# Two score levels of a chunked RWKV-6 kernel computed in 32 by 32 and 64 by 64 blocks of the TensorE array

## The chip, the cores and the metric

The kernel runs on one core of a Trainium2 chip. The metric is the device time of one launch in microseconds; lower is better. The kernel before takes 628.2 us (median of three runs, 627.67 to 628.48). Everything is float32.

## What is computed

The reference is an RWKV-6 attention followed by a small feed-forward block:

```python
# r, k, v, w: (4 batches, 8 heads, 768 tokens, 48)
for t in range(S):
    cur   = einsum('bhd,bhe->bhde', u * k[t], v[t])
    y[t]  = einsum('bhd,bhde->bhe', r[t], state + cur)
    state = w[t] * state + einsum('bhd,bhe->bhde', k[t], v[t])
x   = y, heads side by side            # (3072, 384)
h   = x @ w_in                         # (3072, 2048)
out = (h * sigmoid(h)) @ w_out         # (3072, 384)
```

The recurrence is not run token by token. Inside a chunk of 128 tokens the weight of key j for query t is the product of r[t], k[j] and all decays w between them. The kernel builds the 128 x 128 matrix of these scores level by level. At level l the chunk is cut into blocks of c = 2^l tokens. A block of odd number has its queries scored against the keys of the even block just before it, with queries and keys already multiplied by the decays up to the border between the two blocks. Level 0 and the diagonal come by another way; levels 1 to 6 are matrix products on TensorE.

## The kernel before

**Units.** The work is cut into 12 units, each of 128 tokens of two batches (`units`, six chunks times two pairs of batches). The eight heads of a batch are four pairs (`NP = 4`); of a pair, one head's 48 channels lie in partitions 0 to 47 and the other's in partitions 64 to 111 (the loop `for e in range(2)` with `rows = slice(PD * e, PD * e + D)`). The second batch of a unit is kept with its tokens in reverse order in places, so that the keys of both batches that a level needs stand in one set of 128 columns (`X[l % 2] + p`): even blocks from batch 0, odd positions from the reversed batch 1.

**Scores.** `score_products` (L659 to L673, its product at L669) makes one level. For each pair p and each half e it issues one product: the stationary operand is 48 x 128 (all 128 keys), the moving one 48 x 128 (64 queries of each batch, taken with a stride, since only the odd blocks count). That is eight products for a level. The result is 128 keys x 128 columns, of which only the blocks where key and query block belong together are scores; the rest is thrown away. `keep_masked` (L676 to L680) then writes the wanted elements into `score` with one predicated copy of 128 x 512 on VectorE for each half, four for two levels.

**Bursts.** From the third unit on, two neighbouring levels are computed back to back: `prepare` makes a second copy of the queries ahead, and `burst` (L743) issues level l from the older queries and level l+1 from the newer. `burst(i, 3)` makes levels 3 and 4, `burst(i, 5)` makes levels 5 and 6. `keep_level` (L751) follows for each of the two levels, then `go_on`, which grows keys (GpSimd) and queries (VectorE) for the next step. The results stay in two pairs of PSUM buffers (`p_sc` and `p_m`, in the third unit `p_sc` and `p_o`). `scores` (L682 and after) is the form of the first two units, where levels are made one at a time; it also knows a copy of rectangles in place of a masked one, on ScalarE, for the levels listed in `COPIED` (L698).

**The rest of a unit.** `turn_k` (L781) transposes keys, `y_state` (L794), `y` (L807) and `update` (L821) make the outputs and the new state, `up` (L929) and `quarter` (L995) are the feed-forward products of the units before. `y` reads `score` and so waits for the copies of all levels.

**Order.** The order is written out by hand: `mix(i)` gives groups of attention steps of unit i, and the main loop puts a counted number of feed-forward steps (`downs(i-2) + ups(i-1)`) behind each group. Every engine then runs its own instructions in the order of the code. A float32 product appears in the profile as two pairs of a weight load and a matmul, so eight products of a level are 16 records of each kind.

Of the kernel before, what the change touches and what calls it, by code (L numbers as in the profile page):

```python
# [38 lines left out]
def kernel(  # L39
# [11 lines left out]
    nc = tc.nc  # L51

    B, H, S, D = r.shape
    DM, DF = moe_w_in.shape
    L = 128
    NL = 7
    NB = 2
    NP = H // 2
    PD = 64
    Q = NB * NP  # L60
    NX = Q + 2 * NP
    X = 0, NP + Q
# [5 lines left out]
    NTOK = 2  # L68
# [250 lines left out]
    NSC = 1  # L319
    score = const.tile([128, NSC, 2, Q, L], F32, name="score")  # L320

    masks = {}
    first = {}
    for l in range(NL):
        c, ni = 1 << l, L >> (l + 1)
# [18 lines left out]
    tw, tr, tk, diag, kq, xt = {}, {}, {}, {}, {}, {}  # L344
# [311 lines left out]
        start_keys(i, nc.gpsimd, False)  # L656


    COPIED = (0, 5, 0), (0, 6, 0), (1, 6, 0)  # L659

    def score_products(i, l, queries, sc):
        c, ni = 1 << l, L >> (l + 1)

        for p in range(NP):
            for e in range(2):
                rows = slice(PD * e, PD * e + D)

                apart, r_p, s_p = 2 * (NP - p) - 1, queries[rows, p, :], sc[e][:, p, :]
                nc.tensor.matmul(bass.AP(tensor=s_p.tensor, offset=s_p.offset,  # L669
                                         ap=[s_p.ap[0], [apart * L // 2, 2], [1, L // 2]]),  # L670
                                 lhsT=tk[i][rows, X[l % 2] + p, :],
                                 rhs=bass.AP(tensor=r_p.tensor, offset=r_p.offset + c,
                                             ap=[r_p.ap[0], [apart * L, 2], [2 * c, ni], [1, c]]),  # L673
                                 start=True, stop=True)

    def keep_masked(i, l, e, sc):  # L676
        c, ni = 1 << l, L >> (l + 1)
        dst = score[:, i % NSC, e].rearrange("p (b q) (i s c) -> p b q i s c", b=NB, s=2, c=c)[:, :, :, :, 1, :]
        nc.vector.copy_predicated(out=dst, mask=masks[l][:, :, None].to_broadcast([128, NB, NP, ni, c]),  # L679
                                  data=sc[e].rearrange("p (b q) (i c) -> p b q i c", b=NB, c=c))  # L680

    def scores(i, l, *between):  # L682
        c, ni = 1 << l, L >> (l + 1)

        name = "p_h" if i == 0 and l % 2 == 1 else "p_sc"
        sc = [ps.tile([128, Q, L // 2], F32, name=name, bufs=2) for e in range(2)]
        score_products(i, l, tr[i], sc)
        if i < NTOK and l + 2 < NL:
            odd_keys(i, l + 1)

        def keep(e):
            if (i, l, e) in COPIED:

                for b in range(NB):
                    for x in range(ni):
                        first = 2 * x * c if b == 0 else L - (2 * x + 1) * c
                        rows, columns = slice(first, first + c), slice((2 * x + 1) * c, (2 * x + 2) * c)
                        nc.scalar.copy(out=score[rows, i % NSC, e, b * NP:(b + 1) * NP, columns],  # L698
                                       in_=sc[e][rows, b * NP:(b + 1) * NP, x * c:(x + 1) * c])
                return  # L700
            keep_masked(i, l, e, sc)
# [39 lines left out]
    made = {}  # L741

    def burst(i, l):  # L743

        other = (second[0], "p_o") if i == NTOK else (ps, "p_m")
        for x, (pool, name) in enumerate(((ps, "p_sc"), other)):
            made[i, l + x] = [pool.tile([128, Q, L // 2], F32, name=name, bufs=2) for e in range(2)]
        score_products(i, l, before.pop((i, l)), made[i, l])
        score_products(i, l + 1, tr[i], made[i, l + 1])

    def keep_level(i, l):  # L751
        for e in range(2):
            keep_masked(i, l, e, made[i, l])

    def go_on(i, l):

# [110 lines left out]
    def mix(i):  # L867
# [22 lines left out]
        if i < NPAIR:  # L890
            groups = [[*both(turn, i, "w"), (product, i, 0)],
                      [*both(turn, i, "k"), *both(turn, i, "r"), (odd_ones, i)], [(start_levels, i), (prepare_keys, i, 1)],
                      [(prepare, i, 1), *[(product, i, l) for l in range(1, NL)]],
                      [(burst, i, 1), (keep_level, i, 1)],
                      [(keep_level, i, 2), (go_on, i, 2)],
                      [(prepare, i, 3), (reverse_v, i), (bonus, i, 0)],
                      [(burst, i, 3), (keep_level, i, 3), (bonus_sum, i, 0), (bonus, i, 1), (bonus, i, 2)],
                      [(keep_level, i, 4), (go_on, i, 4), (bonus_sum, i, 1), (load_rk, i + 1), (load_u,)],
                      [(prepare, i, 5), (make_block_mask,), (bonus_spread, i), (bonus_write, i)],
                      [(burst, i, 5), (keep_level, i, 5), (keep_level, i, 6), (go_on, i, 6)], *end]  # L900
        else:
            groups = [[], [(odd_keys, i, 2), (grow_keys, i, 2, False), (grow_queries, i, 2), *sum_steps(i, 2)],
                      [(prepare, i, 3), *bonus_steps(i, 6, 7)],
                      [(burst, i, 3), (keep_level, i, 3), *sum_steps(i, 3, 4), (block_move, i), *at(ahead, (load_rk, i + 1))],
                      [(keep_level, i, 4), (go_on, i, 4)],
                      [(prepare, i, 5), (reverse_v, i)],
                      [(block_spread, i), (block_write, i)],
                      [(burst, i, 5), (keep_level, i, 5), (keep_level, i, 6), (go_on, i, 6)], *end]
# [231 lines left out]
```

## Time and profile before

| | |
|---|---|
| median of the runs | 628.2 us (627.67 to 628.48) |
| the profiled execution | 628.39 us |
| its span | 626.6 us |
| around the span | 1.8 us (628.39 - 626.6) |
| TensorE busy in the span | 620.3 us, 99% |
| VectorE busy | 438.6 us, 70% |
| GpSimd busy | 363.7 us, 58% |
| ScalarE busy | 187.4 us, 30% |
| granted TensorE clock | full, in every slice |

The span is the time from the first to the last instruction that the profiler saw; the launch adds 1.8 us to it. In lists of groups a line holds the source line, the engine, the operation, the tiles written and read, the shape, the number of instructions, their busy time and the mean of one, and the idle time of the engine ahead of them. Matmul records overlap, so the mean duration of one matmul is its latency; its price in a stream is the time of a stretch divided by the number of its matmuls, which the chain of waits gives.

### The profile page before, as it was taken

Reading aid. Unit: us, or ns where it says so; the run is one execution under the profiler, and the core shown is the slowest. Engines: PE = TensorE matmul, PEld = TensorE weight load, DVE = VectorE, ACT = ScalarE, POOL = GpSimd, SP = SyncE. Lnnn points to the kernel's source line nnn. Section 1 sums busy time; section 2 is a strip of 40 time slices with the busy share of each in tenths; the row PEclk is TensorE's granted clock in tenths of the full one; section 3 lists DMA queues with packets and bytes.
Section 4 is the critical chain, followed back from the end, with each engine's and each line's share of the span. In section 5 each row is a group of like instructions: output and inputs, shape, how many; then the busy total and the mean of one; then the engine's idle time right before and its main releaser. Section 6 shows DMA issues by size and latency. Waiting matters only on the chain.

```text
span 626.6 us, 12324 instructions
## 1 busy us (share of the span) xinstructions
PE 620.3 (99%) x4606; PEld 562.8 (90%) x4606; DVE 438.6 (70%) x749; ACT 187.4 (30%) x380; POOL 363.7 (58%) x414
## 2 busy tenths in 40 slices
PE   8999999999999999999999999999999999999997
PEld 8888876799899899899899899889889989989997
DVE  6879779898995694794794595686596596571041
ACT  6798882221321320320320321221221221220110
POOL 6998388566676567567577378378378458400000
PEclk9999999999999999999999999999999999999999
DMA  9966874443543643543543543542542312100000
GB/s 227 291 154 163 164 203 49 88 79 66 101 68 50 133 66 68 106 69 63 105 67 54 110 65 52 115 64 51 115 70 50 77 33 51 35 1 27 25 1 25
DMA packets 203067, 53.25 MB, mean 85 GB/s; under 512 B 186752, under 2 KB 194816, under 8 KB 203008
## 3 DMA queue, kind: packets, MB, share of 16 engines
q1 hardware_dynamic: 201424, 51.88, 41.1%
q10 hardware_dynamic: 1584, 0.59, 0.4%
q8 instruction: 36, 0.59, 0.4%
q14 instruction: 23, 0.19, 0.1%
HBM read 43.21 MB, written 5.24 MB: 77 GB/s over the span
## 4 chain that ended last, share of the span: by engine, by line
PE 94%; POOL 1%; DVE 1%; ACT 1%; DMA 1%; issue 1%; POOLq 0%; ACTq 0%
PE p_h L929 41%; PE p_o L995 32%; PE p_sc L669 5%; PE p_m L951 3%; PE p_m L807 3%; PE p_m L794 3%; PE p_m L669 3%; PE p_m L781 1%; PE p_sc L821 1%; DMA raw<-in_k_dram 1%; PE p_m L372 1%; POOL tk L625 1%; PE p_m L845 0%; DVE score L584 0%; POOL w_in_sb L241 0%
## 5 line engine op out<-in xcount | busy, mean ns | idle before, releaser
L929 PE MATMUL p_h<-xt,w_in_sb 128*128 128x256 f32 x1152 | 258.1, 382 | 0.7 <-POOL tk L649 0.7
L929 PEld LDWEIGHTS p_h<-xt,w_in_sb 128*128 128x128 f32 x1152 | 215.9, 190 | 32.6 <-POOL tk L649 0.9
L938 ACT ACTIVATE gt<-p_h 128x512 f32<-128x512 f32 x90 | 53.7, 597 | 256.1 <-PE p_h L929 255.9
L625 POOL TENSOR_TENSOR tk<-tk,tw 128x256 f32<-128x256 f32 x128 | 88.7, 714 | 62.4 <-ACT tk L595 34.7
L995 PE MATMUL p_o<-own,temps 128*128 128x192 f32 x528 | 87.9, 326 | 0.0
L995 PE MATMUL p_o<-w_out_sb,gt 128*128 128x192 f32 x508 | 87.3, 328 | 0.0
L995 PEld LDWEIGHTS p_o<-own,temps 128*128 128x128 f32 x528 | 86.0, 190 | 0.2
L995 PEld LDWEIGHTS p_o<-w_out_sb,gt 128*128 128x128 f32 x508 | 82.7, 190 | 0.9 <-issue 0.4
L487 POOL TENSOR_TENSOR ruk<-tokens_rk 128x768 f32<-128x768 f32 (+1 forms) x32 | 48.5, 1527 | 46.3 <-DMA tokens_rk<-in_k_dram 33.7
L977 DVE TENSOR_TENSOR temps<-gt 128x256 f32<-128x256 f32 x84 | 55.4, 660 | 18.3 <-ACT gt L938 18.3
L408 POOL TENSOR_TENSOR tw<-tw 128x256 f32<-128x256 f32 (+6 forms) x83 | 43.8, 528 | 40.2 <-DVE tw L360 36.3
L679 DVE COPY_PREDICATED score<-mask,p_sc 128x512 f32<-128x512 int8 x62 | 44.5, 772 | 13.4 <-PE p_sc L669 12.7
L607 DVE TENSOR_TENSOR tr<-tr,tw 128x512 f32<-128x512 f32 x61 | 49.6, 813 | 3.7 <-POOL tk L625 1.1
L595 ACT COPY tk<-tk 128x256 f32<-128x256 f32 x52 | 20.9, 403 | 85.4 <-POOL tk L625 67.1
L1004 DVE TENSOR_TENSOR partial<-p_o,partial 128x192 f32<-128x192 f32 x33 | 11.8, 358 | 47.2 <-PE p_o L995 47.1
L669 PEld LDWEIGHTS p_sc<-tr,tk 48*128 48x128 f32 x512 | 31.4, 187 | 10.3 <-issue 7.3
L669 PE MATMUL p_sc<-tr,tk 48*128 48x128 f32 x512 | 37.7, 285 | 0.7 <-POOL tk L625 0.6
L1004 DVE TENSOR_TENSOR temps<-p_o,partial 128x192 f32<-128x192 f32 x22 | 7.9, 358 | 33.3 <-PE p_o L995 23.1
L995 PE MATMUL p_o<-w_out_sb,temps 128*128 128x192 f32 x176 | 30.4, 326 | 0.0
L995 PEld LDWEIGHTS p_o<-w_out_sb,temps 128*128 128x128 f32 x176 | 28.9, 190 | 0.0
L487 POOL TENSOR_TENSOR tokens_rk<-tokens_rk,tokens_w 128x192 f32<-128x192 f32 (+1 forms) x32 | 26.8, 857 | 1.3
L977 DVE TENSOR_TENSOR temps<-temps,gt 128x256 f32<-128x256 f32 x43 | 25.7, 598 | 1.5
(170 smaller groups left out, 828.0 us busy)
## 6 DMA issues: line engine op xcount, KB each, us to landing
w_out_sb<-in_moe_w_in_dram SPq DMA_DIRECT2D x6, 768.0 KB, 7.0
w_out_sb<-in_moe_w_out_dram SPq DMA_DIRECT2D x4, 768.0 KB, 5.1
own<-in_moe_w_out_dram SPq DMA_DIRECT2D x4, 768.0 KB, 5.1
tokens_rk<-in_r_dram SPq DMA_DIRECT2D x8, 384.0 KB, 4.5
tokens_rk<-in_k_dram SPq DMA_DIRECT2D x8, 384.0 KB, 5.3
tokens_w<-in_w_dram SPq DMA_DIRECT2D x8, 384.0 KB, 6.6
xt<-yt SPq DMA_DIRECT2D x60, 48.0 KB, 2.0
raw<-in_w_dram SPq DMA_DIRECT2D x80, 32.0 KB, 2.3
```

The source lines that it names most:

```text
L408: engine.tensor_tensor(out=up, in0=t[:, :, 0::2], in1=t[:, :, 1::2], op=ALU.mult)
L487: mul = lambda out, one, two: nc.gpsimd.tensor_tensor(out=out, in0=one, in1=two, op=ALU.mult)
L595: nc.scalar.copy(out=keys(i, X[(l + 1) % 2] * L + c, [4 * c, blocks], [c, 2], [1, c]), in_=keys(i, NP * L + c, [4 * c, blocks], [NP * L + ...
L607: nc.vector.tensor_tensor(out=odd, in0=odd, in1=tw[i][l][:, :, 0::2][:, :, :, None].to_broadcast([128, Q, L >> (l + 1), c]), op=ALU.mult)
L625: nc.gpsimd.tensor_tensor(out=out, in0=have, in1=odd_products(i, l, b, *blocks), op=ALU.mult)
L669: nc.tensor.matmul(bass.AP(tensor=s_p.tensor, offset=s_p.offset, ap=[s_p.ap[0], [apart * L // 2, 2], [1, L // 2]]), lhsT=tk[i][rows, X[l % ...
L679: nc.vector.copy_predicated(out=dst, mask=masks[l][:, :, None].to_broadcast([128, NB, NP, ni, c]), data=sc[e].rearrange("p (b q) (i c) -> ...
L929: nc.tensor.matmul(p_h[:, a, :], lhsT=w_in_sb[:, c, f * 128:(f + 1) * 128], rhs=xt[i][:, c, :], start=(c == 0), stop=(c == KC - 1))
L938: nc.scalar.activation(out=gt[i, m], in_=p_h, func=AF.Silu)
L977: nc.vector.tensor_tensor(out=out, in0=one, in1=two, op=op)
L995: nc.tensor.matmul(p, lhsT=left(f), rhs=right[:, f, :], start=(f == 0), stop=(f == FH - 1))
L1004: nc.vector.tensor_tensor(out=to, in0=p, in1=known, op=ALU.add)
```

## The change

For units from the third on and levels from 5 on, `score_products` no longer multiplies all 128 keys with all queries and masks the result. It walks over the blocks of keys (four of 32 at level 5, two of 64 at level 6) and multiplies each with the one block of queries that belongs to it: a stationary operand of 48 x 32 (48 x 64) and a moving one of the same size, written to the 32 (64) partitions of PSUM that belong to these keys. `corner` tells for block x which batch it belongs to and where its tokens begin. The products of level 5 become 32 in place of 8, those of level 6 become 16 in place of 8. `keep_level` no longer calls the masked copy for these levels; since the wanted elements now are rectangles, it copies each rectangle for all four pairs at once: half e = 0 on VectorE, half e = 1 on ScalarE, four copies of 32 x 128 for level 5 and two of 64 x 256 for level 6 on each of the two engines. The first two units and levels 1 to 4 are as they were.

```diff
+    APART = 5
+
+    def corner(l, x):
+
+        return x % 2, x if x % 2 == 0 else (L >> l) - 1 - x
+
     COPIED = (0, 5, 0), (0, 6, 0), (1, 6, 0)
 
     def score_products(i, l, queries, sc):
         c, ni = 1 << l, L >> (l + 1)
+        if i >= NTOK and l >= APART:
+            for p in range(NP):
+                for x in range(L // c):
+                    b, first = corner(l, x)
+                    q = (p, 2 * NP - 1 - p)[b]
+                    for e in range(2):
+                        rows = slice(PD * e, PD * e + D)
+                        nc.tensor.matmul(sc[e][x * c:(x + 1) * c, q, first // 2 * c:(first // 2 + 1) * c],
+                                         lhsT=tk[i][rows, X[l % 2] + p, x * c:(x + 1) * c],
+                                         rhs=queries[rows, q, (first + 1) * c:(first + 2) * c], start=True, stop=True)
+            return
 
         for p in range(NP):
...
     def keep_level(i, l):
+        c = 1 << l
         for e in range(2):
-            keep_masked(i, l, e, made[i, l])
+            if l < APART:
+                keep_masked(i, l, e, made[i, l])
+                continue
+            for x in range(L // c):
+                b, first = corner(l, x)
+                (nc.vector.tensor_copy if e == 0 else nc.scalar.copy)(
+                    out=score[x * c:(x + 1) * c, i % NSC, e, b * NP:(b + 1) * NP, (first + 1) * c:(first + 2) * c],
+                    in_=made[i, l][e][x * c:(x + 1) * c, b * NP:(b + 1) * NP, first // 2 * c:(first // 2 + 1) * c])
```

## The prediction

> **What bounds the kernel now.** I read the page first (busy shares, clock, the chain by engine), then the list of waits of TensorE, then the chain in order of time around the units.
>
> ```profile
> PE 620.3 (99%) x4606; PEld 562.8 (90%) x4606; DVE 438.6 (70%) x749; ACT 187.4 (30%) x380; POOL 363.7 (58%) x414
> PEclk9999999999999999999999999999999999999999
> PE 94%; POOL 1%; DVE 1%; ACT 1%; DMA 1%; issue 1%; POOLq 0%; ACTq 0%
> ```
>
> TensorE (PE) carries 94% of the chain, at full clock. The list of its waits says whether it ever stands still for another engine:
>
> ```profile
> PE p_m L1030 <- POOL ident masks.py:199: 1.4, 1, 1.4
> PE p_h L929 <- POOL tk L649: 0.7, 1, 0.7
> PE p_sc L669 <- POOL tk L625: 0.6, 1, 0.6
> PE p_m L372 <- ACT tr L384: 0.2, 1, 0.2
> PE p_m L372 <- DMA raw<-in_k_dram: 0.2, 1, 0.2
> ```
>
> Five waits, each once, 3.1 us in all, and all in the first two units. From the third unit on, where the change acts, TensorE never waits for data. So the kernel is worth what TensorE's own instructions cost, and time that the change takes out of them leaves the end of the kernel. Their prices come from the chain (start, duration, work; x counts records, two for a product):
>
> ```profile
> 50.36 1.09 PE p_sc L669 x16
> 51.45 2.79 PE p_h L929 x12
> ...
> 456.55 1.09 PE p_sc L669 x16
> 457.64 0.89 PE p_m L669 x16
> 458.54 5.38 PE p_h L929 x24
> 463.91 0.87 PE p_m L781 x8
> 464.79 2.59 PE p_h L929 x12
> 467.38 1.78 PE p_m L794 x16
> 469.16 1.89 PE p_m L807 x32
> 471.05 0.72 PE p_sc L821 x32
> ```
>
> The two L669 lines at 456.55 are the levels 5 and 6 of one unit: 1.09 + 0.89 = 1.98 us. The same pair stands in the chain once for each of the 10 units from the third on. Four readings follow.
> - A record of 256 columns costs 2.59 / 12 = 216 ns, one of 128 (L794) 111 ns: about 0.83 ns a column and 5 ns.
> - Two blocks of the array work side by side. L669 uses the upper and the lower rows in turn: 0.89 / 16 = 56 ns a record, half of 111. L807 and L821 use two groups of output columns in turn: 59 ns for 128 columns, and 0.72 / 32 = 22.5 ns for 48 columns, where one block alone would need 45.
> - A change between shapes of the array costs 0.2 us each way: the first level of a burst takes 1.09 and the second 0.89; twelve L929 records take 2.79 after scores and 2.59 after transposes. In the timeline the next weight load starts about 0.09 us after the last stream before it would have ended, and the first matmul waits about 0.11 us for its 128 columns of weights.
> - Issue. By narrowing the timeline's window, the two records of a pair of blocks start 6 to 7 ns apart (441.348 and 441.355). The sequencer is quicker than any stream here: two of its own waits, both behind an emptied queue, stand at 46.34 and 46.51, with 14 records (28 instructions) between them.
>
> ```profile
> L669 PEldq EVENT_SEMAPHORE  x1: 51/51/51, 46.3 to 46.3; - x1
> L929 PEldq EVENT_SEMAPHORE  x1: 51/51/51, 46.5 to 46.5; - x1
> ```
>
> That is 165 - 51 = 114 ns for 28 instructions, 4 ns each, 8 ns for a weight load and its matmul.
>
> [...]
>
> **The change part by part.** All of it for one unit, times 10.
>
> *Removed on TensorE:* 32 records of L669, 1.98 us.
>
> *Level 5 added:* 32 products, 64 records, 48 x 32 with 32 columns, over 8 blocks (two row groups, four column groups). By the array each block has 8 records of 0.83 x 32 + 5 = 32 ns: 0.26 us. By issue 64 records: at 6.5 ns 0.42 us, at the sequencer's 8 ns 0.51 us, at L821's 22.5 ns 1.44 us. Issue decides. I take 8 ns, 0.51 us, because L821's rate is explained by its 48 columns on two blocks (45 / 2) and so is no issue limit[...]. Ends kept: 6.5 ns below, 16 ns (half of the eight-block overlap lost, 1.02 us) above.
>
> *Level 6 added:* 16 products, 32 records of 64 columns over 4 blocks: 8 in each, 0.83 x 64 + 5 = 58 ns: 0.46 us. Issue at 8 ns would be 0.26 us and hides.
>
> *Edges:* at the entry a drain of 0.09 and a weight load of 32 columns, a quarter of 0.11: 0.12 us. Between the levels the blocks change from quarters to halves of the columns, so there is a new drain: 0.09 + half of 0.11 = 0.15 us[...]. At the exit the L929 records keep their 0.2 us, as before. The wait instructions of 51 ns ahead of level 6 stand in a queue that level 5 has just emptied: 0.05 us that were hidden before.
>
> *Sum:* 0.51 + 0.46 + 0.12 + 0.15 + 0.05 = 1.29 us against 1.98: 0.69 us less a unit, 6.9 us in ten. In the third unit, whose burst lies at 115.7 us where VectorE is at its busiest (digits 9 and 8 in slices 7 and 8 of the page), I count half, since a wait may take the rest: 6.6 us.
>
> *Copies.* The rows that price them (two of line L698, the existing rectangles on ScalarE; two VectorE groups):
>
> ```profile
> L698 ACT COPY score<-p_h x4: 255/257/258, 25.7 to 26.5; 32x128 f32<-32x128 f32 x4
> L698 ACT COPY score<-p_sc x4: 366/367/368, 28.8 to 65.9; 64x256 f32<-64x256 f32 x4
> L679 DVE COPY_PREDICATED score<-mask,p_m 128x512 f32<-128x512 int8 x38 | 25.1, 715 | 0.0
> L837 DVE COPY state<-p_m 48x384 f32<-48x384 f32 x2 | 1.1, 556 | 1.0 <-PE p_m L821 0.9
> ```
>
> ScalarE gains 4 x 257 + 2 x 367 = 1.76 us a unit, in an engine that works 10.8 of 48.8 us. VectorE loses 4 x 0.715 = 2.86 and gains, at about 1.04 ns an element and 0.16 us fixed (from the 384-element copy of 556 ns and the 192-element addition of 358 ns), 4 x 0.29 + 2 x 0.42 = 2.0 us: 0.86 less. Neither lies on the path: the scores are read by `y` at 469.16, more than 10 us after the burst, behind three `up`, the transposes and `y_state`; the SiLU of the `up` before starts at 456.59 and is done when the first rectangle is. Behind ScalarE's new copies, which now wait for the burst and for VectorE's last write to `score` (done at 457.56), stands only the next SiLU, whose matmuls end at 461.3. I cost them at nothing; without that cover it would be 1.8 us a unit. The first pair of PSUM buffers is asked for again by L821 and the second by L781, 5.4 us after the burst; the copies end about 1 us earlier than the masked ones. POOL's and SP's queues keep their instructions and order.
>
> **The rivals.**
> 1. *A floor of issue* (ends slower). If a long run of tiny records holds L821's 22.5 ns, level 5 takes 1.44, level 6 0.72, with edges 2.48 us: 0.50 more a unit, 633.4 us. It decides from about 18 ns a record on: 64 x 18 + 32 x 18 = 1.73 us, and with 0.32 of edges 2.05, past 1.98. For it: nothing here shows more than two blocks, and the number of TensorE instructions in a burst triples, 64 to 192. Against: the 4 ns an instruction above.
> 2. *Overlap of only part of the blocks.* With 16 ns a record at level 5 the sum is 1.80 us, a gain of 1.8 us: 626.6 us.
> 3. *The gain waits elsewhere.* The saved time turns up as a wait of TensorE for GpSimd or VectorE, about 628. Against: no wait after the second unit, and in a unit of 48.7 us VectorE works 35.5 and GpSimd 31.5.
> 4. *The drains are free and the issue is at its best:* 0.42 + 0.46 + 0.12 = 1.00 us, 9.8 us less: 618.6.
>
> **How the numbers follow.** The profiled execution took 628.39 us (span 626.6 and 1.8 around it), 0.2 above the median. 628.39 - 6.6 = 621.8; against the median 621.6 us. Chances: the forecast with its own spread, rival 4 included, 0.78; rival 2 0.08; rival 3 0.05; rival 1 0.09. The range goes from 619.0, near rival 4, to 626.4, near rival 2. Within 0.2% (1.3 us) counts as no change, which is about what a measurement of this kernel can tell; rival 2 lies just beyond it. Faster 0.85, same 0.06, slower 0.09.
>
> **What would show it.** In the chain after the change, each unit's level 5 and level 6 lines should read about 0.6 and 0.65 us in place of 1.09 and 0.89, the L929 lines after them unchanged, and TensorE's waits still all early. Records of level 5 about 8 ns apart confirm the issue step; 20 ns or more refute it. VectorE's busy time should fall by some 9 us and ScalarE's rise by 18. The prediction is wrong if level 5 is bound per instruction, or if the step from level 5 to level 6 costs more than the 0.2 us seen at other edges.

## The result and the profile after

| | before | after |
|---|---|---|
| median of the runs | 628.08 us (627.67 to 628.48) | 622.14 us (621.96 to 623.03) |
| ratio, after to before | | 0.9904 [0.9892, 0.9916] |
| the profiled execution | 628.39 us | 622.15 us |
| its span | 626.6 us | 620.3 us |

The change takes 5.9 us off, 0.96%. The forecast was 621.6 us. The page of the kernel after, busy times and the chain by engine:

```profile
span 620.3 us, 13663 instructions
PE 613.0 (99%) x5246; PEld 555.4 (90%) x5246; DVE 438.5 (71%) x769; ACT 205.1 (33%) x440; POOL 364.5 (59%) x414
PE 93%; DVE 2%; POOL 2%; DMA 1%; ACT 1%; issue 1%; SPq 0%; POOLq 0%; DVEq 0%; ACTq 0%
```

TensorE has 640 matmuls more (5246 against 4606) and is busy 7.3 us less. VectorE, which was to fall, stands still. The chain of waits of the kernel after, at the unit that the prediction showed (start, duration, work; after the change L676 is the product of blocks, L686 the old product, L954 `up`):

```profile
452.31 0.69 PE p_sc L676 x48
453.00 0.62 PE p_m L676 x32
453.62 5.38 PE p_h L954 x24
```

1.09 + 0.89 has become 0.69 + 0.62 = 1.31 us (the chain counts only the records that carry it on, so x48 of 64 at level 5). The lines behind it are as before, to 0.01 us. All ten bursts look like this one, the third unit's too (0.69 and 0.62 at 115.32).

Where did 626.6 - 620.3 = 6.3 us come from? I set the starts of the feed-forward products, which are the same in both kernels, side by side. They move ahead by 0.67 us at each of the ten bursts, 6.7 in all. They were 0.37 us ahead from the loading at the start on, where the two kernels are the same. And they fall back twice, 0.26 us near 139 us and 0.51 us near 186 us (0.05 more at the record behind it): -6.7 - 0.4 + 0.8 = -6.3. The second of these is in TensorE's list of waits of the kernel after (engine, tile and line, what it waited for: total us, times, longest):

```profile
PE p_h L686 <- DVE tr L607: 0.4, 1, 0.4
PE p_o L1020 <- DVE temps L1029: 0.3, 1, 0.3
```

The first line belongs to the start (it lies at 13.5 us); the second is new and late. Its 0.3 us is the time in which no matmul ran at all; from one start to the next it cost 0.51. The chain of waits of the kernel after, around 186 us, follows it back:

```profile
183.26 0.42 DVE state L860
...
183.69 0.70 DVE tr L607
184.39 1.32 DVE block_sums L521 x2
...
185.75 0.37 DVE temps L1029
...
186.16 10.67 PE p_o L1020 x64
```

TensorE's `quarter` asks for a PSUM buffer that VectorE's addition L1029 has to empty, and the addition stands last in a row of VectorE's work that runs on without a pause. The other place is a step further from VectorE. GpSimd's timeline of the kernel after (start, duration, instruction, in brackets its idle time before and who ended it):

```profile
131.55 1.04 POOL L408 TENSOR_TENSOR tw<-tw 128x512 f32<-128x512 f32 x1 [4.95 <-DVE tw L360]
...
136.12 2.81 POOL L625 TENSOR_TENSOR tk<-tk,tw 128x256 f32<-128x256 f32 x2 [0.55 <-ACT tk L595]
```

and the weight loads of TensorE there:

```profile
138.98 0.97 PEld L686 LDWEIGHTS p_m<-tr,tk 48*128 48x128 f32 x16 [0.18 <-POOL tk L625]
```

The second level of that burst needs keys that GpSimd finishes at 138.93, and GpSimd had waited 4.95 us for VectorE's transpose of the decays. In the kernel before GpSimd finished at 139.53 and the loads began at 139.74: 0.2 us of room. TensorE then came 1.0 us earlier (0.37 + 0.67), VectorE's transposes and with them GpSimd only 0.6, so 0.4 of delay less the room of 0.2, which is about the 0.26 seen. The experiment with VectorE's copies moved away, below, tests both readings.

### The profile page after: what moved, and what is told of

Read it like the earlier page. It is cut to its first block, busy times and chain, and to the rows that moved or that the text cites. A ratio compares the mean times of both kernels' runs of the same rounds, so it can differ in the third digit from the quotient of the medians.

```text
span 620.3 us, 13663 instructions
## 1 busy us (share of the span) xinstructions
PE 613.0 (99%) x5246; PEld 555.4 (90%) x5246; DVE 438.5 (71%) x769; ACT 205.1 (33%) x440; POOL 364.5 (59%) x414
## 3 DMA queue, kind: packets, MB, share of 16 engines
q1 hardware_dynamic: 201424, 51.88, 41.2%
## 4 chain that ended last, share of the span: by engine, by line
PE 93%; DVE 2%; POOL 2%; DMA 1%; ACT 1%; issue 1%; SPq 0%; POOLq 0%; DVEq 0%; ACTq 0%
PE p_h L954 41%; PE p_o L1020 32%; PE p_sc L686 3%; PE p_m L976 3%; PE p_m L832 3%; PE p_m L819 3%; PE p_m L686 1%; PE p_m L806 1%; PE p_sc L676 1%; PE p_sc L846 1%; PE p_m L676 1%; DMA raw<-in_r_dram 1%; POOL tk L625 1%; PE p_m L870 0%; DVE score L584 0%
## 5 line engine op out<-in xcount | busy, mean ns | idle before, releaser
L954 PE MATMUL p_h<-xt,w_in_sb 128*128 128x256 f32 x1152 | 258.1, 382 | 0.7 <-POOL tk L649 0.7
L954 PEld LDWEIGHTS p_h<-xt,w_in_sb 128*128 128x128 f32 x1152 | 215.9, 190 | 32.1 <-POOL tk L649 0.9
L487 POOL TENSOR_TENSOR ruk<-tokens_rk 128x768 f32<-128x768 f32 (+1 forms) x32 | 50.0, 1571 | 44.8 <-DMA tokens_rk<-in_k_dram 28.5
L1002 DVE TENSOR_TENSOR temps<-gt 128x256 f32<-128x256 f32 x84 | 53.0, 630 | 18.3 <-ACT gt L963 18.3
L607 DVE TENSOR_TENSOR tr<-tr,tw 128x512 f32<-128x512 f32 x61 | 49.7, 815 | 4.0 <-POOL tk L625 1.1
L1029 DVE TENSOR_TENSOR partial<-p_o,partial 128x192 f32<-128x192 f32 x33 | 11.8, 359 | 44.5 <-PE p_o L1020 44.3
L696 DVE COPY_PREDICATED score<-mask,p_sc 128x512 f32<-128x512 int8 x42 | 31.2, 797 | 6.9 <-PE p_sc L686 6.5
L1029 DVE TENSOR_TENSOR temps<-p_o,partial 128x192 f32<-128x192 f32 x22 | 7.9, 358 | 33.2 <-PE p_o L1020 22.9
L1002 DVE TENSOR_TENSOR temps<-temps,gt 128x256 f32<-128x256 f32 x43 | 28.9, 673 | 1.5
L686 PEld LDWEIGHTS p_sc<-tr,tk 48*128 48x128 f32 x352 | 21.7, 187 | 6.8 <-issue 4.4
L686 PE MATMUL p_sc<-tr,tk 48*128 48x128 f32 x352 | 26.1, 285 | 0.7 <-POOL tk L625 0.6
L754 DVE TENSOR_TENSOR tr<-tr,tw 128x512 f32<-128x512 f32 x21 | 26.5, 1261 | 0.3
```

The source lines that it names most:

```text
L487: mul = lambda out, one, two: nc.gpsimd.tensor_tensor(out=out, in0=one, in1=two, op=ALU.mult)
L607: nc.vector.tensor_tensor(out=odd, in0=odd, in1=tw[i][l][:, :, 0::2][:, :, :, None].to_broadcast([128, Q, L >> (l + 1), c]), op=ALU.mult)
L754: nc.vector.tensor_tensor(out=new[:, :, :, 1, :], in0=old[:, :, :, 1, :], in1=tw[i][l][:, :, 0::2][:, :, :, None].to_broadcast([128, Q, L ...
L954: nc.tensor.matmul(p_h[:, a, :], lhsT=w_in_sb[:, c, f * 128:(f + 1) * 128], rhs=xt[i][:, c, :], start=(c == 0), stop=(c == KC - 1))
L1002: nc.vector.tensor_tensor(out=out, in0=one, in1=two, op=op)
```

## The experiments

Each diff is against the kernel after; the ratio is time over the kernel before, with its 95% interval. The lines of these kernels are numbered anew, so that one product can have another line number in another kernel.

### The copies alone: e1_copies

All products as before the change, the rectangles kept.

```diff
-        if i >= NTOK and l >= APART:
+        if i >= NTOK and l > NL:
```

> Products as before (eight of 48 x 128 for each of levels 5 and 6), the rectangular copies of the change. Theory (the gain is TensorE's alone, the copies lie beside it): level 5 and 6 stay at 1.09 and 0.89 us in the chain, VectorE about 0.9 us less and ScalarE 1.76 us more a unit, time as before, 627.8 to 628.4 us. Rival (part of the gain comes from VectorE's lighter copies): 626 to 627 us.

Measured: 628.36 us, ratio 1.0002 [0.9993, 1.001]; in the chain of waits the old pair of 1.09 and 0.89 us is back. The copies alone are worth nothing, in either direction. The gain is the products'. VectorE's busy time is 438.8 us here too: the 0.9 us a unit that the expectation took off it does not show.

### One level at a time: e2_six and e3_five

Level 6 alone in blocks:

```diff
-    APART = 5
+    APART = 6
```

> Only level 6 in blocks; level 5 as before. Theory (a change of block shape costs about 0.2 us, and with both levels in blocks two of the three changes are paid anyway): level 5 1.09, level 6 0.62 us, 0.27 less a unit, 2.7 in ten, less a little given back in the fourth unit: 625.4 to 625.8 us. Rival (no cost of the change of shape, each level's gain is its own): level 6 0.47, 0.42 a unit, about 624 us.

Level 5 alone in blocks:

```diff
-        if i >= NTOK and l >= APART:
+        if i >= NTOK and l == APART:
...
-            if l < APART:
+            if l != APART:
                 keep_masked(i, l, e, made[i, l])
```

> Only level 5 in blocks; level 6 as before. Theory: level 5 0.69, level 6 1.09 us (it now has a change of shape ahead of it), 0.20 less a unit: 626.0 to 626.4 us; together with level 6 alone 0.47 a unit, less than the 0.67 of both. Rival (no cost of the change of shape): level 5 0.69, level 6 0.89, 0.40 less a unit, about 624.2 us.

Measured: level 6 alone 627.18 us, ratio 0.9984 [0.9977, 0.999]; level 5 alone 626.59 us, 0.9976 [0.9967, 0.9985]. The chain of waits with level 6 alone:

```profile
455.94 1.09 PE p_sc L686 x16
457.03 0.62 PE p_m L676 x32
```

and with level 5 alone:

```profile
455.45 0.69 PE p_sc L676 x49
456.13 1.09 PE p_m L686 x16
```

Alone, level 6 saves 0.27 us a unit and level 5 saves 0.21 (from the starts of the products behind the bursts), together 0.48, where both at once save 0.67. The missing 0.2 is the change of shape: with level 5 alone the old level 6 costs 1.09 in place of 0.89, since it now follows a level of another shape. That is the price of an edge read off before, now seen where the edit puts an edge.

The time of level 5 alone is 0.2 us above the expected range. The time of level 6 alone misses its expectation by more, though its bursts are right to the hundredth: 2.7 us should have come out of ten units, and 1.2 us was given back in three places. The largest, 0.67 us near 128 us, is on ScalarE. The chain of waits of that kernel:

```profile
119.65 1.26 DVE score L696 x2
...
120.99 0.36 ACT score L776
...
121.74 0.60 ACT gt L963
...
123.29 0.48 ACT kq L807
...
123.81 2.05 PE p_m L819 x16
```

ScalarE's rectangles of level 6 write into `score` behind VectorE's masked copies of level 5, so ScalarE stands until 120.99; behind it in its queue stand the SiLU (`gt`) and the copies of keys (`kq`) for which `y_state` (L819) then waits. The prediction named this queue and took its cover as enough. In the kernel after the masked copies of level 5 are gone, and with them this wait.

### The order of the products: e4_order

The same 32 and 16 products, with the pair p innermost, so that four products in a row (eight records) go to the same block of the array.

```diff
-            for p in range(NP):
-                for x in range(L // c):
-                    b, first = corner(l, x)
-                    q = (p, 2 * NP - 1 - p)[b]
-                    for e in range(2):
+            for x in range(L // c):
+                for e in range(2):
+                    for p in range(NP):
+                        b, first = corner(l, x)
+                        q = (p, 2 * NP - 1 - p)[b]
```

> The same products in another order: block of keys outermost, then half, then the four pairs, so that four products in a row need the same block of the array. Theory[...]: two blocks at a time, level 5 64 x 16 = 1.02 + 0.12 us, level 6 32 x 29 + 0.15 = 1.08 us, 2.2 a unit, 628 to 631 us. Rival (issue alone sets the pace, 16.7 ns a product whatever the block): 622 us as the change.

Measured: 637.25 us, ratio 1.0144 [1.0129, 1.0159]. The chain of waits of this kernel:

```profile
462.99 1.44 PE p_sc L676 x64
464.43 1.47 PE p_m L676 x32
```

2.91 us a burst, 1.60 more than in the kernel after and 0.93 more than before the change. The number of instructions is the same, so a price per instruction cannot be what makes it. Between most starts of records stand gaps of 26 to 32 ns at level 5 and 52 to 59 ns at level 6, near the price of one block alone (32 and 58 ns). On the mean a record takes 20.6 ns at level 5, (1.44 - 0.12) / 64, and some 41 at level 6, where two blocks side by side would give 16 and 29. With the turn through the blocks, in the kernel after, it is 8.8 and some 15 ns: the turn makes the rate, and more of it is lost without the turn than the expectation allowed for (2.2 us a burst). The edit changes one thing beside the block: eight records in a row also write to one of the level's two PSUM buffers, where the kernel after goes from one to the other at each product. No run separates the two; against the buffer speaks L821 of the kernel before, whose records all write to one buffer and yet come 22.5 ns apart on two blocks, where one block alone would need 45.

### The price of issue: e9_twice

The products of level 5 are issued twice, the second time over the same results.

```diff
-            for p in range(NP):
+            for p in [p for p in range(NP) for again in range(2 if l == 5 else 1)]:
```

> Each product of level 5 is issued twice (the second writes the same result again): 64 products, 128 records. Theory (issue of 4.2 ns an instruction, 8.35 ns a record, is the bound of level 5): 0.53 us more a unit, level 5 at 1.22 us, 627.0 to 627.8 us. Rival (a bound of the array, 32 ns for each record of a block, eight side by side): 0.26 more a unit, 624.7 us; a floor of 22.5 ns a record in a long run: 1.4 more a unit, 636 us.

Measured: 636.55 us, ratio 1.0128 [1.0109, 1.0148]. The chain of waits in a usual burst of this kernel:

```profile
465.20 1.22 PE p_sc L676 x80
466.42 0.62 PE p_m L676 x32
```

In eight of the ten units 64 more records cost 1.22 - 0.69 = 0.53 us, 8.3 ns a record or 4.2 ns an instruction. That settles the issue step: the array's own price would have added 0.26, a floor of 22.5 ns a record 1.4. The time alone would have misled: it lies at the 636 us that the expectation gave to the floor. It is 14.4 us above that of the kernel after, 9 more than ten times 0.53, because in two bursts TensorE stood still. The same view at the first of them:

```profile
162.38 0.50 PE p_m L676 x23
162.88 2.94 issue
165.82 0.58 PE p_m L676 x8
```

TensorE stands for 2.9 us in the middle of a level, and "issue" means that the trace shows nothing it waited for. The second burst has the same:

```profile
220.20 1.81 issue
```

The list of DMA queues of this kernel, between 162.8 and 163.2 us (queue, packets, MB, share of the 16 engines' time; whole packets are counted, so the share can pass 100%):

```profile
q1 hardware_dynamic: 46, 0.11, 111.4%
q8 instruction: 1, 0.02, 20.1%
```

The DMA engines are full with loads of data, and a packet on the queue of instructions lies in the stall, from 163.08 to 164.36 us. The page of the kernel after gives that queue 0.67 MB in 41 packets, 16 KB each, and both instruction queues 0.86 MB for 13663 instructions, 63 bytes each. By these figures one packet is, as an estimate, some 260 instructions, and a doubled burst has 320. At the second stall the packet lies otherwise: it runs from 219.16 to 220.47 us, so that most of it is ahead of the stall, and the DMA engines are not full. The same list between 219.9 and 222 us:

```profile
q1 hardware_dynamic: 672, 0.06, 24.6%
```

What both stalls share is that TensorE goes on about 1.5 us after the end of such a packet. Whether it stood for want of instructions is not shown; the full DMA engines can have a part in the first stall alone. All this is inferred from things that lie together; no run separated them.

After the two stalls some 12 and 8 records of `up` start 427 ns apart where 216 is usual, 0.21 us more each; the granted clock of these stretches is 0.50. The two bursts are 3.8 and 2.1 us longer than the other eight, and the slow records cost 2.6 and 1.6 us: 10.1 in all. The 0.8 us that the kernel after loses behind VectorE is not lost here, which leaves about the 9 us.

### Other shapes of the blocks: e5_six32 and e6_half5

Level 6 as 32 keys by 64 queries, so that it keeps the block shape of level 5 (32 products in place of 16):

```diff
-                        nc.tensor.matmul(sc[e][x * c:(x + 1) * c, q, first // 2 * c:(first // 2 + 1) * c],
-                                         lhsT=tk[i][rows, X[l % 2] + p, x * c:(x + 1) * c],
-                                         rhs=queries[rows, q, (first + 1) * c:(first + 2) * c], start=True, stop=True)
+                        for k0 in range(x * c, (x + 1) * c, 32):
+                            nc.tensor.matmul(sc[e][k0:k0 + 32, q, first // 2 * c:(first // 2 + 1) * c],
+                                             lhsT=tk[i][rows, X[l % 2] + p, k0:k0 + 32],
+                                             rhs=queries[rows, q, (first + 1) * c:(first + 2) * c], start=True, stop=True)
```

> Level 6 in blocks of 32 keys by 64 queries, 32 products in place of 16, so that levels 5 and 6 use the same shape of blocks. Theory (the pause between the levels, 0.12 us with 0.05 of weight load, is the change of shape): level 6 64 records at 8.4 ns = 0.54 us and no pause, 0.08 less a unit than the change: 621.0 to 621.6 us. Rival (the pause has another cause, such as the wait ahead of level 6): 0.54 + 0.15 = 0.69, 0.07 more a unit: 622.5 to 623.2 us.

Level 5 as 64 keys by 32 queries of each batch, so that it takes the shape of level 6 (16 products in place of 32):

```diff
+        if i >= NTOK and l == 5:
+            for p in range(NP):
+                for h in range(2):
+                    for e in range(2):
+                        rows = slice(PD * e, PD * e + D)
+                        apart, r_p, s_p = 2 * (NP - p) - 1, queries[rows, p, :], sc[e][64 * h:64 * h + 64, p, :]
+                        nc.tensor.matmul(bass.AP(tensor=s_p.tensor, offset=s_p.offset + 32 * h,
+                                                 ap=[s_p.ap[0], [apart * 64 + (1 - 2 * h) * 32, 2], [1, 32]]),
+                                         lhsT=tk[i][rows, X[l % 2] + p, 64 * h:64 * h + 64],
+                                         rhs=bass.AP(tensor=r_p.tensor, offset=r_p.offset + 64 * h + c,
+                                                     ap=[r_p.ap[0], [apart * L + (1 - 2 * h) * 64, 2], [2 * c, ni // 2], [1, c]]),
+                                         start=True, stop=True)
+            return
```

> Level 5 in 16 products of 64 keys by 2 x 32 queries (half of each result is not used), the shape of level 6's blocks. Theory: 32 records over four blocks at 58 ns each block, 0.47 us, entry 0.12, no pause ahead of level 6, 0.47 us more: about 1.08 a unit in place of 1.31, 2.3 us less in ten: 619.5 to 620.5 us, a little less gain if the waits of the fourth unit grow. Rival (the multiplications count, not the records and changes of shape): level 5 slower than in quarters, 623 us or more.

Measured: with blocks of 32 keys at both levels 624.39 us, ratio 0.9949 [0.9929, 0.997]; with blocks of 64 keys at both 621.88 us, 0.9897 [0.9882, 0.9912]. The chain of waits of the first:

```profile
454.74 0.69 PE p_sc L677 x48
455.42 0.70 PE p_m L677 x48
```

and of the second:

```profile
451.77 0.62 PE p_sc L675 x32
452.40 0.47 PE p_m L689 x32
```

In both, the gap between the last start of level 5 and the first of level 6 falls, from 123 ns to 44 (in nine of ten bursts) and to 38. In the second the stream of level 6 shrinks too, from 476 ns to 428, as its first four records no longer stand ahead of a gap of their own. So the line of level 6 goes from 0.62 to 0.47. The wait instruction of 51 ns ahead of level 6, which the expectation names as another cause, is still there in both kernels: the change of shape between the levels costs 0.15 us (0.62 less 0.47), and the gap that the prediction put there is real. Drain is the prediction's word for it; the trace shows its length alone. In the first kernel the gain is paid back at once, because level 6 now has 64 records, which take 632 ns in place of 476. Its time lies some 3 us above the expectation. Half of that is level 6, 0.70 us a burst where 0.54 was expected; why its 64 records take 632 ns is open, since 64 at 8.4 ns would be 540. The rest is given back in waits, the largest of 1.35 us near 236 us behind VectorE. The second is the better form, 0.62 + 0.47 = 1.09 us a burst, 2.2 us less than the kernel after in ten. But its time cannot be told from that of the kernel after (the intervals overlap): some 1.9 us came back as waits at 128, 140, 187 and 236 us, where the expectation of 619.5 to 620.5 us had left room for little. The list of waits puts those at 187 and 236 to VectorE.

### VectorE's share: e7_halves and e10_act

Levels 3 and 4 too in halves of the array, in the way of the last diff, from the third unit on (the condition is `3 <= l <= 5`). Their masked copies must then leave out what is not computed, eight of 64 x 128 in place of two of 128 x 512 a level:

```diff
+            if 3 <= l < APART:
+                ni = L >> (l + 1)
+                for h in range(2):
+                    for b in range(NB):
+                        rows, at = slice(64 * h, 64 * h + 64), (h, 1 - h)[b] * ni // 2
+                        nc.vector.copy_predicated(
+                            out=score[rows, i % NSC, e, b * NP:(b + 1) * NP].rearrange(
+                                "p q (i s c) -> p q i s c", s=2, c=c)[:, :, at:at + ni // 2, 1, :],
...
+                continue
```

> Levels 3, 4 and 5 in 16 products of 64 keys by 2 x 32 queries each, level 6 as in the change; the masked copies of levels 3 and 4 in eight pieces of 64 x 128 in place of two of 128 x 512, since half of the result isn't written. Theory (TensorE alone bounds): burst of levels 3 and 4 from 1.98 to about 1.08 us, 0.9 less in each of ten units on top of the half-level variant: 611 to 613 us. Rival (VectorE, with 1.7 us more a unit, takes over): TensorE waits for VectorE or GpSimd, 614 to 620 us.

All rectangles of levels 5 and 6 on ScalarE, none on VectorE:

```diff
-                (nc.vector.tensor_copy if e == 0 else nc.scalar.copy)(
+                nc.scalar.copy(
```

> The change with all its rectangles copied by ScalarE, none by VectorE. Theory (what the change gives back, 0.26 us at the unit near 139 us and 0.51 us near 186 us, is TensorE waiting for VectorE, which is busy without pause from 161 to 186 us): VectorE has about 2 us less a unit, both waits go, 621.2 to 621.6 us. Rival (VectorE is late there because its own inputs come late): both waits stay, 622.1 us.

Measured: halves for levels 3 to 5, 620.09 us, ratio 0.9873 [0.9849, 0.9898]; rectangles on ScalarE, 621.66 us, 0.99 [0.9887, 0.9914]. With the halves every pair of bursts is at its best, but some 8 us come back in the third to fifth units, and the time lies at the upper end of the rival's range. The longest entry of TensorE's waits in that kernel:

```profile
PE p_o L1045 <- DVE temps L1054: 3.9, 3, 2.2
```

This and another of 1.2 us are VectorE's, and that kernel gives VectorE more to do. About 1.5 us of the 8 are of another kind: behind a stop near 115 us seven records of `up` start 427 ns apart in place of 216, at a granted clock of 0.50. The other experiment turns it round. Busy time by engine in the stretch from 161 to 186 us (columns: the stretch, its length, then busy us and instructions of PE, PEld, DVE, ACT and POOL, granted clock, DMA share, GB/s), in the kernel after:

```profile
161.00:186.00 25.00, 24.81 (x248) 22.94 (x245) 24.66 (x38) 7.33 (x17) 15.94 (x18) 1.00 0.52 92
```

and with the rectangles on ScalarE:

```profile
161.00:186.00 25.00, 25.00 (x220) 23.23 (x217) 21.89 (x34) 8.77 (x22) 16.78 (x19) 1.00 0.50 85
```

In this stretch VectorE had 0.34 us of 25 free in the kernel after. With the rectangles gone it is busy 2.8 us less in the same stretch, and TensorE is busy throughout. GpSimd's first step of the other place begins at 130.84 in place of 131.55, and TensorE's level there takes its usual 0.89. The first delay is gone, and of the second 0.40 of the 0.51 us; 0.11 us is left at 185.3 us, too short for the list of waits. A delay of 0.27 us near 234 us, behind the same addition of VectorE, was not in the kernel after; the kernel with the copies alone has it too, near 236 us. So 0.66 of the 0.77 us is shown to hang on VectorE's work. In time the move cannot be told from the kernel after: 0.5 us of span in one execution, of which 0.2 us lies at the loading.

### Put together: e11_half5_act, e12_late and e13_late_act

The halves for level 5 with all rectangles on ScalarE:

> Level 5 in 16 products of 64 keys, and all rectangles copied by ScalarE. Theory: ten times 0.89 us less than the kernel before, with only a little given back: 619.0 to 619.9 us. Rival (the waits stay whatever the copies): 621.9 us, as the same products with the copies shared.

Levels 3 and 4 in halves only from the sixth unit on, where VectorE has room; level 5 in halves from the third; rectangles shared between VectorE and ScalarE:

```diff
+        if i >= NTOK and (l == 5 or i >= 5 and 3 <= l < 5):
...
+            if i >= 5 and 3 <= l < APART:
```

> Level 5 in 16 products of 64 keys in all ten units, levels 3 and 4 so as well from the sixth unit on, copies shared between VectorE and ScalarE. Theory (VectorE bounds only the third to fifth unit; later it has room for 1.7 us more): 0.89 us less in each of the seven late units, about 0.8 given back: 615.8 to 617.2 us. Rival (VectorE's extra copies take the gain in the late units too): 619.5 to 622 us.

The same with all rectangles on ScalarE:

> As the variant with levels 3 and 4 in halves from the sixth unit on, and all rectangles of levels 5 and 6 copied by ScalarE. Theory: both gains add, 613.0 to 614.8 us. Rival (no gain from the copies' engine): as the variant with shared copies.

| | median us | ratio |
|---|---|---|
| level 5 in halves, rectangles on ScalarE | 620.25 (620.05 to 620.64) | 0.9876 [0.9863, 0.989] |
| levels 3 and 4 from the sixth unit | 615.29 (614.61 to 615.49) | 0.9793 [0.9779, 0.9806] |
| the same, rectangles on ScalarE | 614.94 (613.85 to 615.28) | 0.9788 [0.9774, 0.9801] |

The last two beat both kernels, and cannot be told from each other, so in the last the rival holds: beside the late halves, ScalarE's copies bring nothing that the times show. The middle one is half a microsecond better than expected. The first is 0.35 us above its range; it gains 0.89 us a unit, of which 1.1 us in all comes back. The chain of waits of the last, at a burst of levels 3 and 4:

```profile
480.50 0.62 PE p_sc L675 x32
481.12 0.47 PE p_m L675 x32
```

Both bursts of a unit now take 1.09 us, and from the sixth unit on all of it is kept. What still comes back, 1.7 us, is in the stretch up to 236 us. The chain of the last kernel there:

```profile
219.59 0.45 SPq L109
220.08 1.79 DMA raw<-in_k_dram
...
224.09 1.20 DVE tr L360 x2
...
234.63 0.37 DVE temps L1054
235.04 10.02 PE p_o L1045 x60
```

The chain goes back from VectorE's row of work to a load, and from the load to SP's queue (SPq), which issues the loads one by one, 0.45 us each. That is where a next change would have to start; it wasn't tried. Products in blocks with the masked copies kept were not tried either, because the masked copy reads parts of PSUM that the blocks don't write.

## Why the prediction was right, step by step

**TensorE's own instructions set the end.** Held, but for the 0.8 us of waits: 0.67 us less in each burst moved all that came after by 0.67, and the lines between bursts kept their durations.

**Level 5, 0.51 by issue plus 0.12 at the entry, 0.63.** Measured 0.69: the mean pace was nearly right, but the burst is uneven. Weight loads of one burst in the kernel after, in slices of 0.1 us (columns: the slice, its length, busy us and loads under way, clock, DMA share, GB/s):

```profile
452.30:452.40 0.10, 0.10 (x33) 1.00 0.00 0
452.40:452.50 0.10, 0.10 (x22) 1.00 0.00 0
452.50:452.60 0.10, 0.10 (x10) 1.00 0.02 3
452.60:452.70 0.10, 0.10 (x21) 1.00 0.34 34
```

A load lasts about 106 ns, so a slice counts some that began in the one before. The count dips in the slice from 452.5. Taken matmul by matmul, the first 32 start 5.3 ns apart on the mean (31 gaps, 163 ns), then come gaps of 78 and 31 ns, and the other 30 gaps take 292 ns, 9.7 each: most of these records start in pairs 17 ns apart, which is 8.3 a record, and a few singly. 163 + 109 + 292 make the 564 ns from the first start to the last. Against the 8 ns of the prediction the first half is 85 ns ahead, the pause costs 93 and the second half 52, which is the error of 0.06 us. The pause stands behind the 32nd record in all ten bursts, and in the doubled level 5 too, where 128 follow one another; what it is stays open.

**Level 6, 0.46 plus 0.15 and 0.05, 0.66.** Measured 0.62. Without the change of shape the line takes 0.47, so the stream and the gap between the levels were sized right (0.46 and 0.15), and the 0.05 us for the wait instructions was not there to be paid. The 0.15 was an estimate from the edges of the bursts before; the 123 ns from the last start of level 5 to the first of level 6, against 38 without the change of shape, bear it out. The two errors of size, +0.06 and -0.04, leave 1.31 for 1.29.

**The third unit at half.** Wrong in place and too small. That unit kept its whole 0.67. The loss came later, 0.26 us near 139 and 0.51 near 186, behind VectorE as feared. The step took off 0.3 us and the runs showed 0.8. The luck of 0.37 us at the loading makes up for it in the profiled execution; ten bursts less the 0.77 are 6.0 us, which is what the medians show (5.9). The forecast gain of 6.6 us was too large by 0.7, of which this step is 0.5 and the burst (0.67 in place of 0.69) 0.2.

**Copies at nothing.** Held where the products are as before: the kernel with the copies alone takes the time of the kernel before. Beside the faster products it does not hold to the end, since moving VectorE's share to ScalarE took away 0.66 us of the delay. VectorE's prices, from L776 in the kernel after (duration ns, smallest, median and largest):

```profile
L776 DVE COPY score<-p_sc x40: 264/286/297, 119.2 to 548.5; 32x128 f32<-32x128 f32 x40
L776 DVE COPY score<-p_m x18: 417/422/429, 164.1 to 549.2; 64x256 f32<-64x256 f32 x18
```

The estimates of 290 and 420 ns on VectorE were right, and ScalarE rose by 17.7 us (18 forecast). VectorE did not fall by 9 us: 438.6 became 438.5. Added up record by record, the masked copies lost 28.8 us and the rectangles brought 19.8, the forecast 9. But `tr` at the preparation of a burst grew from 1113 to 1261 ns each and one form of `temps` from 598 to 673, 3 us each in all, while another fell by 2.5. So the sum of durations fell by 4.2 us, from 483.9 to 479.7. Busy time counts the records that overlap once, and their overlap fell by 4.1 us too, from 45.3 to 41.2; so nothing is left. Why some run longer was not separated.

**The rivals.** The floor of issue falls: 64 records more cost 8.3 ns each in a level of 128. The overlap of only some blocks falls for this order, and the experiment on the order shows that it was the order that kept it off. The gain waiting elsewhere was true in part, 0.8 us of 6.7; "TensorE's waits still all early" was wrong for one line of the list.

## What to carry to other kernels

Small products that fill a part of the array cost, in these runs, about the larger of two times: the records that fall on one block, at that block's price (58 ns for 64 columns), and all records at the pace of issue (8.3 ns). For level 6 and for level 5 in halves that is 8 x 58 = 464 ns (476 and 477 measured from first start to last), for level 5 in quarters 64 x 8.3 = 531 (564), for the doubled one 1062 (1097). For level 6 in blocks of 32 keys it is 531 and 632 were measured, so a tenth of a microsecond can be missing. To get it, write the loops so that neighbouring products fall on different blocks, which was worth 1.6 us a burst here, and put products of one shape behind one another, which was worth 0.15 us between levels 5 and 6. When one engine carries the chain and a second is full for some stretch, look for that stretch before adding up the gain: what is saved there can come back (0.8 of 6.7 us here), and the same edit made only where the second engine has room (from the sixth unit on) kept all of it there.

## What was not expected of the hardware

- A pause of about 0.1 us (78 + 31 ns) after exactly 32 records of level 5, whether it has 64 records or 128. With level 6 in 64 records, a smaller one (35 and 28 ns) comes after 32 of them in eight of the ten bursts.
- The order of the products counts more than the number of blocks in use: with eight records in a row on a block the rate at level 5 is 20.6 ns, where turning through the blocks gives 8.8 (0.564 / 64). Eight blocks without the turn (1.44 us) are slower than two with it (1.09 in the kernel before).
- A dense run of instructions can stand still where the trace shows nothing that it waits for: 2.9 and 1.8 us in two of ten doubled bursts. Each time it went on about 1.5 us after the end of a packet of instructions, and the granted clock after them was 0.50 for some 5 and 3.5 us.
